# Retention of blocks 4 to 35 by chunks of 64 tokens, with quadrants of TensorE and a stacked operand for values and state

## The chip, the cores and the metric

The program runs on one core of a Trainium2 chip. A core has TensorE (PE in the profile: matmuls, with weight loads listed apart as PEld), VectorE (DVE), ScalarE (ACT), GpSimd (POOL) and SyncE (SP), which issues the DMA transfers here. Each engine runs its own instruction stream and waits for others by semaphores. The metric is the time of one execution on the device in microseconds (us); the time of a version is the median of several runs.

## The reference, cut to what matters

```python
# q, k, v: (8 batches, 8 heads, 576 tokens, 64)
scores = scale * np.matmul(q, k.transpose(0, 1, 3, 2))
gamma = 1.0 - 2.0 ** (-5.0 - np.arange(H))             # one decay for each head
Dmat = np.where(rel >= 0, gamma[:, None, None] ** rel[None, :, :], 0.0)   # rel = row - column
attn = np.matmul(scores * Dmat[None], v)
x = attn.transpose(0, 2, 1, 3).reshape(4608, 512)      # all heads of a token side by side
h = np.maximum(np.maximum(x @ w1, x @ w2), x @ w3)     # 512 -> 768, three times
out = h @ w_out                                        # 768 -> 512
```

The first part, retention, is linear attention with a decay: a block of tokens can be computed from scores within the block and from a state, the decayed sum of K^T V of all earlier tokens of the sequence, 64x64 for each head. The second part is a feed-forward network (FFN) with a maximum of three products.

## The kernel before

The 4608 tokens are 36 blocks of C = 128 tokens; four blocks make a tile of 512, and there are nine tiles. While the FFN of tile t runs, the retention of tile t + 1 is worked off between its products. The FFN of tile 0 is plain (its weights are being converted meanwhile). From tile 1 on, most of it is a fast matrix multiplication with fewer products and more additions: 20 products for each column block of 128 of the hidden layer (`up`), and seven for the output (`downs`). The names A to E are accumulating banks; a copy of the running sum is taken after most products.

A sequence has 576 tokens, four and a half blocks, so a block can hold the end of one sequence and the start of the next; masks with a zeroed corner and sliced operands take care of that. `start_of(g)` is the row at which a new sequence begins in block g.

The retention of a block (H = 8 heads, NP = 4 pairs of heads, D = 64; `half(j)` is partitions 64j to 64j + 63; `ps_r` is a pool of four PSUM banks):

```python
def decay_values(g):
    t = vds[g] = vpool.tile([C, H, D], FP32, tag="vd", name="vd")
    nc.gpsimd.tensor_tensor(t[:], raws.pop(("v", g))[:], gk[:].unsqueeze(2).to_broadcast([C, H, D]),
                            op=ALU.mult)
def transposes(g):
    both = qks[g] = {}
    if g >= BY_PE:
        for n in ("k", "q"):
            t = both[n] = att.tile([P, NP, C], FP32, tag=n + "T", name=n + "T", bufs=2 if n == "k" else 3)
            soon(partial(nc.vector.transpose, t[:].rearrange("a p c -> a (p c)"),
                         raws.pop(("kx" if n == "k" else n, g))[:].rearrange("a p b i -> a (p b i)")))
        return
    for n, src in (("k", raws["k", g]), ("q", raws.pop(("q", g)))):
        pool, tag = (ps_r, "r") if g >= CPT else (ps_x, "x")
        pt = pool.tile([P, NP, C], FP32, tag=tag, name=n + "t")
        for p in range(NP):
            nc.tensor.transpose(pt[:, p, :], pair(src, p), ident[:C, :C])
        t = both[n] = att.tile([P, NP, C], FP32, tag=n + "T", name=n + "T", bufs=2 if n == "k" else 3)
        nc.scalar.copy(t[:], pt[:])
def scores(g):
    chore(len(urgent))
    qT, kT = qks[g]["q"], qks[g]["k"]
    s = [ps_r.tile([C, NP, C], FP32, tag="r", name=f"s{j}") for j in range(2)]
    for p in range(NP):
        for j in range(2):
            r = slice(D * j, D * (j + 1))
            nc.tensor.matmul(s[j][:, p, :], lhsT=kT[r, p, :], rhs=qT[r, p, :], start=True, stop=True)
    st = sts[g] = att.tile([C, 2, NP, C], FP32, tag="st", name="st", bufs=2)
    for j in range(2):
        soon(partial(nc.vector.tensor_tensor, st[:, j], s[j][:],
                     masks[start_of(g)][:].unsqueeze(1).to_broadcast([C, NP, C]), op=ALU.mult))
def state(g):
    kr = raws["k", g]
    kvs[g] = None
    if begins(g):
        r = start_of(g) or 0
        kvs[g] = ps_r.tile([P, NP, D], FP32, tag="r", name="kv")
        for h in range(H):
            nc.tensor.matmul(kvs[g][half(h % 2), h // 2, :], lhsT=kr[r:, h, :], rhs=vds[g][r:, h, :],
                             start=True, stop=True)
def keep(g):
    def step(t, kv):
        if start_of(g) is not None:
            nc.vector.tensor_tensor(t[:], kv[:], gs[:], op=ALU.mult)
        else:
            nc.vector.tensor_tensor(t[:], kv[:], states[g][:], op=ALU.add)
            nc.gpsimd.tensor_tensor(t[:], t[:], gs[:], op=ALU.mult)
    if begins(g):
        t = states[g + 1] = stp.tile([P, NP, D], FP32, tag="state", name="state")
        soon(partial(step, t, kvs[g]))
def values(chunks, new_states=(), later=False):
    def before(g):
        return C if start_of(g) is None else start_of(g)
    chore(len(urgent))
    t, i = divmod(chunks[0], CPT)
    pool, tag = (ps_r, "r") if chunks[0] >= CPT - 1 else (ps_y, "y")
    o = [pool.tile([P, len(chunks), NP // 2, C], FP32, tag=tag, name="o") for _ in range(2)]
    for m, g in enumerate(chunks):
        for n in range(NP):
            for c in range(2):
                h = head(c, n)
                nc.tensor.matmul(o[n % 2][half(c), m, n // 2, :], lhsT=vds[g][:, h, :],
                                 rhs=sts[g][:, h % 2, h // 2, :], start=m == 0 and n < 2,
                                 stop=before(g) == 0, skip_group_check=True)
    for g in new_states:
        if g not in kvs:
            state(g)
    for m, g in enumerate(chunks):
        old = before(g)
        if old > 0:
            for n in range(NP):
                for c in range(2):
                    h = head(c, n)
                    r = half(h % 2)
                    nc.tensor.matmul(o[n % 2][half(c), m, n // 2, :old], lhsT=states[g][r, h // 2, :],
                                     rhs=qks[g]["q"][r, h // 2, :old], start=False, stop=True,
                                     skip_group_check=True)
    finish = partial(output, chunks, o, t, i)
    if later:
        return finish
    finish()
    for g in new_states[:1]:
        if g >= CPT:
            keep(g)
```

`soon` puts a step into a queue, `urgent`, that is worked off one step at a time between FFN products, so that VectorE and ScalarE work is spread. `chore(len(urgent))` empties it. When the steps of a tile are due is set here (twelve steps make a tile):

```python
for n in range(0, CPT, 2):
    a, b, m = CPT * t + n, CPT * t + n + 1, 6 * (n // 2)
    at(m, (keep, a), (transposes, b), (decay_values, b))
    ...
    at(m + 2, (scores, a), (scores, b))
    at(m + 3, (decay_values, a + 2))
    at(m + 4, (values, [a, b], [b, a + 2]), (transposes, a + 2), (load, a + 4))
```

The products of the FFN that surround the retention, with what ScalarE and VectorE do after each:

```python
PRODUCTS = """E a11 b12, E a14 b42, B s15 n5, A a22 b21, C s3 b23, B s19 b41, A s10 b32, C a13 b31, B s6 n2, A s13 b22,
              C a11 b11, B s14 n1, A s11 n4, D s7 b43, B a23 n6, A s20 b33, D s16 b13, B a21 n3, A a21 n8, A a24 n7"""
...
def up(t, h, fb):
    lo, hi = h[:, fb, 0:NH], h[:, fb, NH:NT]
    ps, of = {}, {}
    def join(out, a, b, op=ALU.add):
        nc.vector.tensor_tensor(out, a, b, op=op)
    def after(step):
        if step not in ("E1", "E2", "C2", "C3", "A6", "B5"):
            t = of[step] = ppool.tile([P, NH], FP32, tag="part", name="part")
            nc.scalar.copy(t[:], ps[step[0]][:])
        for out, ins, op in JOINS.get(step, ()):
            ins = [ps[n[0]] if n in ("E", "C") else of[n] for n in ins]
            join({"lo": lo, "hi": hi}.get(out) if out in ("lo", "hi") else of[out][:],
                 *(x[:] for x in ins), op)
    done = {}
    for chain, x, w in PRODUCTS:
        n = done[chain] = done.get(chain, 0) + 1
        if n == 1:
            pool, tag = (ps_x, "x") if chain in "AB" else (ps_y, "y")
            ps[chain] = pool.tile([P, NH], FP32, tag=tag, name=chain.lower())
        while x not in made[t]:
            chore()
        ends = n == sum(c == chain for c, _, _ in PRODUCTS)
        nc.tensor.matmul(ps[chain][:], lhsT=factor(w, fb), rhs=xS[t][x], start=n == 1, stop=ends,
                         skip_group_check=True)
        after(f"{chain}{n}")
        yield
...
            elif step % 2 or step % 5 == 4:
                chore(len(urgent) > 0)
```

## Time and profile before

| | |
|---|---|
| median of 3 runs | 775.69 us (775.1 to 776.63) |
| span of the profiled execution | 773.3 us |
| TensorE busy | 766.8 us, 99% |
| VectorE busy | 564.1 us, 73% |
| ScalarE busy | 325.9 us, 42% |
| GpSimd busy | 102.9 us, 13% |
| DMA | 59.33 MB, mean 77 GB/s |

The profile is of one execution. Its page gives each engine's busy time, the span in 40 slices, the DMA queues, the chain of work that ended last, and the costliest groups of instructions. Views of the trace show instructions in order of time: start in us, duration in us, engine, source line, operation, output and inputs by their names in the program, and in brackets how long the engine stood before it and what released it. An "x" and a number are instructions taken together. An fp32 matmul of the program is two records (MATMUL, with two LDWEIGHTS). Matmuls are pipelined, so durations overlap, and what a stretch costs is read from start to start. A shape as 64*128 before the output's is the part of the array that a product uses, rows by columns.

### The profile page before, as it was taken

Reading aid. Unit: us, or ns where it says so; the run is one execution under the profiler, and the core shown is the slowest. Engines: PE = TensorE matmul, PEld = TensorE weight load, DVE = VectorE, ACT = ScalarE, POOL = GpSimd, SP = SyncE. Lnnn points to the kernel's source line nnn. Section 1 sums busy time; section 2 is a strip of 40 time slices with the busy share of each in tenths; the row PEclk is TensorE's granted clock in tenths of the full one; section 3 lists DMA queues with packets and bytes.
Section 4 is the critical chain, followed back from the end, with each engine's and each line's share of the span. In section 5 each row is a group of like instructions: output and inputs, shape, how many; then the busy total and the mean of one; then the engine's idle time right before and its main releaser. Section 6 shows DMA issues by size and latency. Waiting matters only on the chain.

```text
span 773.3 us, 14511 instructions
## 1 busy us (share of the span) xinstructions
PE 766.8 (99%) x5032; PEld 626.5 (81%) x5032; DVE 564.1 (73%) x1249; ACT 325.9 (42%) x811; POOL 102.9 (13%) x124
## 2 busy tenths in 40 slices
PE   9999999999999999999999999999999999999998
PEld 8545454688888888888888888888888888888887
DVE  3898989799577856784768757876778568845672
ACT  3665631163254415451346234532544054514551
POOL 2210021111110201111111111110112001200000
PEclk9999999999999999999999999999999999999999
DMA  9995544333333332333233333333333323001001
GB/s 225 241 226 131 158 110 103 59 58 58 92 58 58 57 77 62 56 75 67 62 56 58 59 96 58 57 58 96 58 56 59 84 48 74 3 15 42 2 1 55
DMA packets 237083, 59.33 MB, mean 77 GB/s; under 512 B 217937, under 2 KB 235729, under 8 KB 237009
## 3 DMA queue, kind: packets, MB, share of 16 engines
q1 hardware_dynamic: 236432, 58.07, 34.9%
q8 instruction: 39, 0.64, 0.3%
q10 hardware_dynamic: 576, 0.33, 0.1%
q14 instruction: 36, 0.29, 0.1%
HBM read 48.89 MB, written 9.44 MB: 75 GB/s over the span
## 4 chain that ended last, share of the span: by engine, by line
PE 97%; SPq 1%; DVE 1%; DMA 1%; issue 0%; ACT 0%; DVEq 0%
PE a L588 18%; PE b L588 16%; PE dx L428 11%; PE up L611 11%; PE c L588 8%; PE dz L428 5%; PE d L588 5%; PE e L588 5%; PE s L243 4%; PE o L299 4%; PE down L598 3%; PE dy L428 3%; PE o L312 2%; PE kv L263 2%; SPq L210 1%; DMA qraw<-in_q_dram 1%
## 5 line engine op out<-in xcount | busy, mean ns | idle before, releaser
L568 DVE TENSOR_TENSOR part<-part 128x256 f32<-128x256 f32 x460 | 208.7, 462 | 78.2 <-ACT part L573 70.4
L573 ACT COPY part<-b 128x256 f32<-128x256 f32 x230 | 85.6, 372 | 126.0 <-PE b L588 114.6
L573 ACT COPY part<-a 128x256 f32<-128x256 f32 x276 | 102.7, 372 | 84.9 <-PE a L588 72.3
L214 POOL TENSOR_TENSOR vd<-vraw,gk 128x512 f32<-128x512 f32 x36 | 40.3, 1120 | 339.2 <-DMA vraw<-in_v_dram 219.9
L611 PE MATMUL up<-xT,w 128*128 128x512 f32 (+2 forms) x200 | 84.7, 578 | 0.3 <-DVE w L517 0.3
L588 PE MATMUL a<-s,w 128*128 128x256 f32 x276 | 82.3, 380 | 0.0
L588 PE MATMUL b<-s,n 128*128 128x256 f32 x276 | 82.1, 379 | 0.0
L611 PEld LDWEIGHTS up<-xT,w 128*128 128x128 f32 x200 | 36.8, 190 | 42.3 <-issue 39.2
L588 PEld LDWEIGHTS b<-s,n 128*128 128x128 f32 x276 | 52.4, 190 | 7.1
L588 PEld LDWEIGHTS a<-s,w 128*128 128x128 f32 x276 | 52.3, 190 | 7.3 <-issue 0.2
L588 PE MATMUL c<-xT,w 128*128 128x256 f32 x184 | 56.0, 386 | 0.0
L588 PE MATMUL b<-xT,n 128*128 128x256 f32 x184 | 55.4, 382 | 0.0
L588 PE MATMUL d<-s,w 128*128 128x256 f32 x184 | 55.1, 381 | 0.0
L568 DVE TENSOR_TENSOR h<-part 128x256 f32<-128x256 f32 x92 | 42.6, 463 | 6.6
L588 PE MATMUL e<-xT,w 128*128 128x256 f32 x184 | 47.3, 379 | 0.0
L588 PE MATMUL a<-xT,n 128*128 128x256 f32 x184 | 47.2, 379 | 0.0
L428 PE MATMUL dx<-To,H 128*128 128x256 f32 (+1 forms) x204 | 44.9, 370 | 0.0
L435 ACT COPY part<-dx 128x256 f32<-128x256 f32 (+1 forms) x34 | 10.5, 363 | 80.1 <-PE dx L428 77.9
L178 DVE TENSOR_TENSOR xT<-o,gq 128x512 f32<-128x512 f32 x28 | 18.1, 686 | 33.3 <-PE o L312 33.3
L428 PEld LDWEIGHTS dx<-To,H 128*128 128x128 f32 x204 | 36.6, 190 | 5.5 <-issue 1.0
L243 PEld LDWEIGHTS s<-qT,kT 64*128 64x128 f32 x576 | 33.9, 188 | 7.9 <-PE b L588 4.0
L272 POOL TENSOR_TENSOR state<-state,gs 128x256 f32<-128x256 f32 x24 | 18.6, 776 | 162.1 <-DVE state L271 162.1
(104 smaller groups left out, 1299.8 us busy)
## 6 DMA issues: line engine op xcount, KB each, us to landing
bits<-in_moe_w_dram SPq DMA_DIRECT2D x36, 256.0 KB, 5.6
out_dram<-osb SPq DMA_DIRECT2D x35, 256.0 KB, 2.1
kraw<-in_k_dram SPq DMA_DIRECT2D x32, 256.0 KB, 3.0
vraw<-in_v_dram SPq DMA_DIRECT2D x32, 256.0 KB, 3.4
qraw<-in_q_dram SPq DMA_DIRECT2D x464, 16.0 KB, 1.8
kxraw<-in_k_dram SPq DMA_DIRECT2D x464, 16.0 KB, 1.8
bits<-in_moe_w_out_dram SPq DMA_DIRECT2D x6, 512.0 KB, 4.7
qraw<-in_q_dram SPq DMA_DIRECT2D x6, 256.0 KB, 4.1
```

The lines of the kernel that those rows point to most:

```text
L178: (urgent or chores).popleft()()
L214: nc.gpsimd.tensor_tensor(t[:], raws.pop(("v", g))[:], gk[:].unsqueeze(2).to_broadcast([C, H, D]), op=ALU.mult)
L243: nc.tensor.matmul(s[j][:, p, :], lhsT=kT[r, p, :], rhs=qT[r, p, :], start=True, stop=True)
L263: nc.tensor.matmul(kvs[g][half(h % 2), h // 2, :], lhsT=kr[r:, h, :], rhs=vds[g][r:, h, :], start=True, stop=True)
L272: nc.gpsimd.tensor_tensor(t[:], t[:], gs[:], op=ALU.mult)
L299: nc.tensor.matmul(o[n % 2][half(c), m, n // 2, :], lhsT=vds[g][:, h, :], rhs=sts[g][:, h % 2, h // 2, :], start=m == 0 and n < 2, stop=be ...
L428: nc.tensor.matmul(o, lhsT=hS[n](fp)[:, m * P:(m + 1) * P], rhs=late["T"][n][:, fp, cols], start=first and fp == 0 and (m == 0 or last and ...
L568: nc.vector.tensor_tensor(out, a, b, op=op)
L573: nc.scalar.copy(t[:], ps[step[0]][:])
L588: nc.tensor.matmul(ps[chain][:], lhsT=factor(w, fb), rhs=xS[t][x], start=n == 1, stop=ends, skip_group_check=True)
L598: nc.tensor.matmul(b[:], lhsT=h[:, fb, m * P:(m + 1) * P], rhs=w_sb["out", fb], start=(fb == 0), stop=(fb == NF - 1))
L611: nc.tensor.matmul(ps[:, cols], lhsT=w_sb[i, fb][:, dc * P:(dc + 1) * P], rhs=xT[t][:, dc, cols], start=dc == 0 and cols.start == 0, stop= ...
```

## The change

Blocks 0 to 3 are computed as before. From block 4 on, a block is two chunks of 64 tokens, so that 576 tokens are nine chunks and a sequence begins only at a chunk's border.

- K^T V of a chunk and its scores are products of 64 by 64 with 64 columns: the four kinds (two chunks, K^T V or scores) fall into the four quadrants of TensorE's array, by the partitions in which operands and outputs lie. GpSimd scales K by the decay, where it scaled V before, and the decay of the scores is in the mask.
- V and the state are stacked: a tile `va` holds a chunk's 64 rows of V in one half of the partitions and the state before it in the other. A tile `m` holds the masked scores in one half and the transposed q in the other. One product of 128 rows then gives the values: 16 products with 64 columns a block, where there were 8 + 8 with 128 columns and the K^T V apart.
- V is loaded straight into its half of the stack. The running state is written into the other half of the next chunk's tile by VectorE (a sum of 64x512), by ScalarE where a sequence begins, and scaled by GpSimd at the end of a block.
- From block 7 on, the transposed q of both chunks comes out of one VectorE transpose into `m1`, and ScalarE copies the half that belongs to chunk 0 into `m0`. For blocks 4 to 6 TensorE transposes, and ScalarE copies the parts.
- Blocks of q and k for the transposes are loaded with all eight heads in one transfer, where two transfers took four heads each.

It is meant to cut TensorE's work for retention. The diff, cut to its core (cuts are marked; blank lines, the loads of V through the old path, the set-up of the first blocks and the schedule of tile 1 are left out):

```diff
             if 0 in blocks:
-                raws[n, g] = raw.tile([P, NP, C // 32, 32], FP32, tag=n, name=n + "raw", bufs=2)
+                raws[n, g] = raw.tile([P, H, 2, 32], FP32, tag=n, name=n + "raw", bufs=2)
             t = raws[n, g]
             for blk in blocks:
                 b, pos = divmod(g * C + 32 * blk, S)
-                for a in range(4):
+                c, e = divmod(blk, 2)
+                for a in range(2):
+                    r = D * (1 - c) + 32 * a
                     nc.sync.dma_start(
-                        t[32 * a:32 * a + 32, :, blk, :],
-                        src[b, a // 2::2, pos:pos + 32, 32 * (a % 2):32 * (a % 2) + 32].rearrange("p j i -> j p i"))
+                        t[r:r + 32, :, e, :],
+                        src[b, :, pos:pos + 32, 32 * a:32 * a + 32].rearrange("h p i -> p h i"))
+    def load_values(g):
+        for c in range(2):
+            t = stacked(g, c)
+            b, pos = divmod(g * C + D * c, S)
+            nc.sync.dma_start(t[half(c)], v[b, :, pos:pos + D, :].rearrange("h p d -> p h d"))
...
-    def decay_values(g):
-        t = vds[g] = vpool.tile([C, H, D], FP32, tag="vd", name="vd")
-        nc.gpsimd.tensor_tensor(t[:], raws.pop(("v", g))[:], gk[:].unsqueeze(2).to_broadcast([C, H, D]),
-                                op=ALU.mult)
+    def decay(g):
+        factor = gk[:].unsqueeze(2).to_broadcast([C, H, D])
+        if g < CPT:
+            t = vds[g] = vpool.tile([C, H, D], FP32, tag="va1", name="vd")
+            nc.gpsimd.tensor_tensor(t[:], raws.pop(("v", g))[:], factor, op=ALU.mult)
+            return
+        nc.gpsimd.tensor_tensor(raws["k", g][:], raws["k", g][:], factor, op=ALU.mult)
+        for c in range(2):
+            if place(g, c) == 0:
+                nc.gpsimd.memset(vas[g, c][half(1 - c)], 0.0)
...
     def transposes(g):
         both = qks[g] = {}
+        if g >= CPT:
+            kT = both["k"] = att.tile([P, H, D], FP32, tag="kT", name="kT", bufs=2)
+            m0, m1 = (att.tile([P, H, D], FP32, tag=f"m{c}", name=f"m{c}", bufs=3) for c in range(2))
+            ms[g, 0], ms[g, 1] = m0, m1
         if g >= BY_PE:
-            for n in ("k", "q"):
-                t = both[n] = att.tile([P, NP, C], FP32, tag=n + "T", name=n + "T", bufs=2 if n == "k" else 3)
-                soon(partial(nc.vector.transpose, t[:].rearrange("a p c -> a (p c)"),
-                             raws.pop(("kx" if n == "k" else n, g))[:].rearrange("a p b i -> a (p b i)")))
+            for n, t in (("kx", kT), ("q", m1)):
+                soon(partial(nc.vector.transpose, t[:].rearrange("a h c -> a (h c)"),
+                             raws.pop((n, g))[:].rearrange("a h b i -> a (h b i)")))
+            soon(partial(nc.scalar.copy, m0[half(1)], m1[half(1)]))
             return
...
+    def chunk_scores(g):
+        kT, kr = qks[g]["k"], raws.pop(("k", g))
+        sk = [ps_r.tile([P, H, D], FP32, tag="r", name=f"sk{j}") for j in range(2)]
+        for h in range(H):
+            for c in range(2):
+                if place(g, c) < S // D - 1:
+                    nc.tensor.matmul(sk[c][half(c), h, :], lhsT=kr[half(c), h, :], rhs=vas[g, c][half(c), h, :],
+                                     start=True, stop=True)
+            for c in (1, 0):
+                r = half(1 - c)
+                nc.tensor.matmul(sk[1 - c][half(c), h, :], lhsT=kT[r, h, :], rhs=ms[g, c][r, h, :],
+                                 start=True, stop=True)
+        def mask(c):
+            nc.vector.tensor_tensor(ms[g, c][half(c)], sk[1 - c][half(c)], gm[half(c)], op=ALU.mult)
+        def keep_chunk(c):
+            to = stacked(g + c, 1 - c)
+            if place(g, c) == 0:
+                nc.scalar.copy(to[half(c)], sk[c][half(c)])
+            else:
+                nc.vector.tensor_tensor(to[half(c)], sk[c][half(c)], vas[g, c][half(1 - c)], op=ALU.add)
+            if c:
+                nc.gpsimd.tensor_tensor(to[half(1)], to[half(1)],
+                                        gs_of[half(1)].unsqueeze(2).to_broadcast([D, H, D]), op=ALU.mult)
+        for c in range(2):
+            if place(g, c) < S // D - 1:
+                soon(partial(keep_chunk, c))
+            soon(partial(mask, c))
...
+                o = [pool.tile([P, 2, NP // 2, C], FP32, tag=tag, name="o")]
+                for m in range(2):
+                    for n in range(NP):
+                        for c in range(2):
+                            h = head(c, n)
+                            nc.tensor.matmul(o[0][half(c), n % 2, n // 2, half(m)], lhsT=vas[g, m][:, h, :], rhs=ms[g, m][:, h, :],
+                                             start=m == 0 and n == 0, stop=True, skip_group_check=True)
...
             a, b, m = CPT * t + n, CPT * t + n + 1, 6 * (n // 2)
-            at(m, (keep, a), (transposes, b), (decay_values, b))
+            at(m, (transposes, b), (decay, b))
             if a == 2 * CPT:
                 at(m, (load, a + 2))
-            at(m, (load, b + 2))
-            at(m + 2, (scores, a), (scores, b))
-            at(m + 3, (decay_values, a + 2))
-            at(m + 4, (values, [a, b], [b, a + 2]), (transposes, a + 2), (load, a + 4))
+            at(m + 2, (scores, a), (scores, b), (load, b + 2))
+            at(m + 3, (decay, a + 2))
+            at(m + 4, (values, a, b), (transposes, a + 2), (load, a + 4))
         return todo
```

## The prediction

> **What bounds the kernel now.** I read the page first: engine totals, then the slices, then the chain that ended last.

> ```profile
> PE 766.8 (99%) x5032; PEld 626.5 (81%) x5032; DVE 564.1 (73%) x1249; ACT 325.9 (42%) x811; POOL 102.9 (13%) x124
> ...
> PEclk9999999999999999999999999999999999999999
> ...
> PE 97%; SPq 1%; DVE 1%; DMA 1%; issue 0%; ACT 0%; DVEq 0%
> ```

> TensorE is busy for 99% of the span at full clock and carries 97% of the chain. In this state any TensorE work removed comes off the time, and any wait put on TensorE is added to it, because there is no slack there. VectorE at 73% has slack on average only.

> Next I read the timeline in a tile in the middle of the run. It shows what retention costs TensorE. First the scores of two chunks, and the first FFN product after them:

> ```profile
> 302.24 2.06 PE L243 MATMUL s<-qT,kT 64*128 64x128 f32 x32
> 304.23 0.70 PE L588 MATMUL c<-xT,w 128*128 128x256 f32 x2
> ```

> Start to start, the scores of a pair of blocks take 304.23 - 302.24 = 1.99 us. Then the values step of the same pair:

> ```profile
> 316.08 1.97 PE L299 MATMUL o<-st,vd 128*64 128x128 f32 x32
> 317.88 0.63 PE L263 MATMUL kv<-vd,kraw 128*64 128x64 f32 x16
> 318.44 1.10 PE L312 MATMUL o<-qT,state 64*64 64x128 f32 x32
> 319.47 0.70 PE L588 MATMUL b<-xT,n 128*128 128x256 f32 x2
> ```

> 319.47 - 316.08 = 3.39 us, with one K^T V left out at the end of a sequence. With both K^T V (1.03 us for 32 records, from 357.32 to 358.35 in the next pair) it is 1.80 + 1.03 + 1.03 = 3.86 us. I take 3.65 us as the mean of the 16 pairs. Every program matmul is two records here.

> [...]in the 64*128 form the 32 score records start 57 ns apart, and the first full product comes about 0.15 us later than that pace. [...]one copy that waits holds up all copies behind it. [...]The trace has 681 ns for 128x512[...]; I use 681 for 64x512 too.[...]

> **The change part by part, on TensorE.** Values: 16 products of 128x64 with 64 columns per block, 64 records a pair, of the same form as K^T V today. At 27.5 ns a record (16 records in 0.41 us from first to last start, 32 in 0.88) that is 1.76 us, and 0.15 us for the exit: 1.9 us. Against 3.65 us this saves 1.75 us a pair, 28 us in 16 pairs.

> Scores and K^T V: 32 products of 64x64 with 64 columns per block, four quadrants in turn, 128 records a pair (a few fewer at sequence ends). What a record costs is read from a pair in which 16 of 32 state records have 64 columns, against a block of 16 with 128 columns:

> ```profile
> 440.42 0.90 PE L312 MATMUL o<-qT,state 64*64 64x64 f32 x32
> 441.25 2.86 PE L428 MATMUL dx<-To,H 128*128 128x256 f32 x12
> ```

> ```profile
> 358.35 0.67 PE L312 MATMUL o<-qT,state 64*64 64x128 f32 x16
> 358.95 2.86 PE L428 MATMUL dx<-To,H 128*128 128x256 f32 x12
> ```

> 0.83 us less 0.60 us leaves 0.23 us for 16 records of 64 columns, 14.4 ns each. 128 x 14.4 = 1.84 us and 0.15 us exit make 2.0 us, what the scores cost now; for a longer run of records I allow +0.1 us a pair, 2 us in all. TensorE's own work thus falls by about **26 us**, and alone this would give 750 us.

> **VectorE, GpSimd, DMA.** The masks stay 64 instructions of 681 ns. 49 running sums (64x512, 681 ns, 33.4 us) replace some 28 of 409 ns (11.5 us): +22 us over 640 us. From 290.6 to 350.4 us, the FFN's up products, VectorE is busy for 45.8 of 59.8 us; four more microseconds fit. The scores of the second block of a pair do not wait for the sums of the first (the stack's halves are tracked apart), and the values come some 14 us after the scores, so this chain is hidden. GpSimd's scaling moves from V to K, 1.04 us as before. Q and K blocks come in half as many, twice as large transfers: hidden.

> **What is put on the path.** For each block from 7 on, VectorE transposes q into m1, and then ScalarE copies 64x512 of it to m0. In the changed program's ScalarE order these 29 copies stand amid the copies of FFN partial products, and TensorE's next product in the same bank waits for those. VectorE runs late just there, at the joins that end an FFN column block. For the third block of a tile, m0's copy stands directly ahead of the copy of the first b:

> ```profile
> 323.03 0.59 PE L588 MATMUL b<-s,n 128*128 128x256 f32 x2
> ...
> 323.66 0.37 ACT L573 COPY part<-b 128x256 f32<-128x256 f32 x1 [0.92 <-PE b L588]
> ...
> 324.33 0.59 PE L588 MATMUL b<-s,w 128*128 128x256 f32 x2
> ...
> 325.95 0.70 DVE L178 STREAM_TRANSPOSE qT<-qraw 128x512 f32<-128x512 f32 x1
> ```

> The transpose ends at 326.62 (the next VectorE instruction starts at 326.57). Now the copy of b at 323.66 has to wait for it: 326.62 + 0.05 + 0.61 (m0) + 0.37 (b) + 0.05 = 327.7, where the second b started at 324.33. **TensorE stands for 3.35 us.** VectorE's order from 321.48 on is the same before and after in this tile, so I take its time over.

> For the fourth block m0's copy stands behind the copy of c and ahead of that of the second b:

> ```profile
> 333.16 0.37 ACT L573 COPY part<-c 128x256 f32<-128x256 f32 x1
> ...
> 334.25 0.59 PE L588 MATMUL b<-s,n 128*128 128x256 f32 x2
> ...
> 335.25 0.42 DVE L269 TENSOR_TENSOR state<-kv,gs 128x256 f32<-128x256 f32 x1
> ...
> 336.54 0.67 DVE L178 STREAM_TRANSPOSE qT<-qraw 128x512 f32<-128x512 f32 x1
> ```

> The transpose ends at 337.2, less 0.33 for the state instruction that goes: 336.9. 336.9 + 0.05 + 0.61 + 0.37 + 0.05 = 337.95 against 334.25 for the third b: 3.7 us. The second block of a tile (transposed at its start, q at 374.92) gives 0.6 us in the same way, the first none, as ScalarE is idle then.

> The sum: third block 6 x 3.35 = 20 us (in the first Strassen tile the copy stands seven products ahead of the one that needs it, so I count none there), fourth block 7 x 3.7 = 26 us, second block 6 x 0.6 = 4 us, and 1 us for the copies of blocks 7 to 9: **50 us of waiting**. 775.7 - 26 + 50 = 800 us.

> **The rivals.** *The copies are harmless:* if VectorE reached the transposes 3 us sooner than in the old trace, the 26 us would show, 750 us. For it: fewer VectorE instructions stand in the pop order ahead of the fourth block's transpose. Against it: the joins that delay it wait for the last products of their column block and are unchanged, and the old trace has nothing idle between 321.48 and 326.62. *Quadrants at 64 columns do not keep 14 ns:* at 25 ns a record a pair costs 1.4 us more, 22 us in all, making 820 us with the waits and 772 without. Only one block of 16 records speaks for 14 ns. *VectorE becomes the bound:* a burst of eight 681 ns instructions (5.5 us) after the scores could delay the join that frees the bank of c. Counted from the scores' end, that join is done about 4.7 us later (with GpSimd's scaling between two sums), and the bank is needed after 5.6 us: it fits with 0.9 us to spare; if not, up to 1 us a pair more, 10 to 15 us.

> **Range and chances.** The two larger terms have opposite signs. The values' saving is safe to 3 us, the scores to 6 us, the waits to 10 us (a shift of 0.8 us in VectorE's lateness times 13 places). Together about 12 us: 784 to 815 us for 8 in 10. Slower by over 2% begins at 791.2 us, 9 us below the middle: 0.72. Faster by over 2% needs the waits to be nearly absent: 0.08. The rest, 0.20, is within 2%.

> **What would show it.** In the changed profile: values of a pair in 1.9 us and scores in 2.0 to 2.1 us start to start; in each tile two gaps of 3 to 4 us on TensorE, whose releaser is a ScalarE copy of b, with ScalarE idle before the m0 copy and its releaser VectorE's transpose of q. The waits of ScalarE on VectorE should rise by some 50 us, and TensorE's busy share fall to about 94%. If those gaps are under 1 us, the prediction fails, and the time is near 750 us; if the scores take 3 us or more, it fails upward.

## The result, and the profile after

The changed kernel takes **834.6 us** (median; 833.2 to 840.5) against 775.4 us (775.1 to 776.6) for the kernel before on the same chip: ratio 1.077, 95% interval 1.074 to 1.081. The direction was predicted, the size was not: 800 us was expected, 784 to 815 us allowed.

The page of the changed kernel, its engine totals and the granted clock in 40 slices:

```profile
PE 770.2 (93%) x6040; PEld 615.9 (74%) x6040; DVE 597.9 (72%) x1270; ACT 352.1 (42%) x869; POOL 121.8 (15%) x138
...
PEclk9999999999999999999998999999999999899999
```

TensorE's busy share fell from 99% to 93%, and the clock has two 8s where before it had none. Its mean is 0.973 of full speed. A clock of 0.973 over 831.5 us is some 45 us at half speed, or 22 us of work lost.

The waits by engine (time in all, times, longest, in us) name the stops:

```profile
ACT m L175 <- DVE m L175: 41.3, 20, 4.0
...
PE b L645 <- ACT part L630: 37.8, 21, 3.3
```

ScalarE waits 41.3 us with its copy m0<-m1 (recorded at line 175) for VectorE's transpose, and TensorE 37.8 us ahead of products of b for ScalarE's copies of b. One such place in the timeline (start, duration, what; in brackets the idle time before it and who ended it), third block of a tile:

```profile
339.72 0.59 PE L645 MATMUL b<-s,n 128*128 128x256 f32 x2
...
342.63 0.70 DVE L175 STREAM_TRANSPOSE m<-qraw 128x512 f32<-128x512 f32 x1
...
343.37 0.61 ACT L175 COPY m<-m 64x512 f32<-64x512 f32 x1 [3.94 <-DVE m L175]
344.01 0.37 ACT L630 COPY part<-b 128x256 f32<-128x256 f32 x1
...
344.43 0.70 PE L645 MATMUL b<-s,w 128*128 128x256 f32 x2 [3.26 <-ACT part L630]
```

Transpose, m0's copy, b's copy, next product of b: TensorE stood for 3.26 us. The product of b before it had ended at 340.31 us and ScalarE was idle from 339.43 us on, yet b's copy began at 344.01, behind m0's. Then something that the prediction does not have: of the products that follow, one starts at 346.21 and the next at 347.06 us, 0.85 us apart instead of 0.43. The table of stretches of 1 us (length, TensorE's busy time and instructions, **granted clock**, DMA share, GB/s) shows why:

```profile
344.00:345.00 1.00, 0.57 (x3) 1.00 0.33 51
345.00:346.00 1.00, 1.00 (x5) 0.72 0.39 60
346.00:347.00 1.00, 1.00 (x3) 0.50 0.48 73
...
349.00:350.00 1.00, 1.00 (x6) 1.00 0.46 71
```

The clock stays at 1.00 through this stop, falls to 0.50 a good microsecond after work has come back, and stays there for 3.4 us (the two stretches left out have 0.50 and 0.57). TensorE paid twice for this stop: in 3.26 us of idle time, and then in 3.4 us at half speed. The expectations below reckon with about 3.3 us at half clock after each stop, an estimate from this one.

Not every stop is followed by half clock. In this profile every stretch at half clock lasts 3.41 or 6.83 us, and all ten begin at multiples of 3.41 us from one another: they lie on one raster. Here are two stops of the same length, 3.26 us, from 254.96 and from 431.86 us on, in a table whose stretches are laid on that raster:

```profile
253.28:256.69 3.41, 1.68 (x8) 1.00 0.00 0
256.69:260.11 3.42, 1.89 (x9) 1.00 0.24 37
```

```profile
430.77:434.18 3.41, 1.09 (x6) 1.00 0.00 0
434.18:437.60 3.42, 2.48 (x6) 0.50 0.33 53
```

The first stop is split into 1.73 and 1.53 us of idle time, and the clock stays, in the stretch after these too. The second has 2.32 us in one stretch, and the clock is halved for the next two. In this profile each full-clock stretch of the raster with 2.13 us or more of idle time is followed by half clock, and none with 1.73 us or less; in number 4 below the border lies between 1.72 and 1.98 us. Elsewhere the border is not sharp: in number 10, of two stretches with 2.0 us of idle time each (ahead of b's products at 260.92 and 273.44 us), only the second is followed by half clock, and in the start of number 14 one with 1.00 us is (a stop of 1.09 us ends at 33.55 us; five records of 512 columns from 35.63 us on take 0.79 us each, the next eleven 0.43 us). This is read off the profiles; no run set the place of a stop on purpose.

To size both I added up TensorE's timeline, start to start, over five tiles (from the first dy product of the third tile to that of the eighth, dy being a bank of the output's products; in us; fourth and fifth column from experiments below):

| | before | changed | copies on GpSimd | before + copies |
|---|---|---|---|---|
| values, K^T V of before | 36.7 | 20.2 | 20.2 | 36.7 |
| scores, K^T V of changed | 19.9 | 20.6 | 20.4 | 19.8 |
| FFN's up products | 262.4 | 283.0 | 263.3 | 283.8 |
| FFN's down products | 91.6 | 91.9 | 91.9 | 91.6 |
| TensorE idle | 0.0 | 35.5 | 5.2 | 30.3 |
| sum | 410.6 | 451.1 | 400.9 | 462.2 |

The up products are the same instructions in every column. They take 20.6 us longer in the changed kernel. Of these tiles' ten stops over 2 us (five of 3.26, five of 2.32), eight are followed by half clock, 34.1 us in all; 31.8 us of it fall on up products and cost half of that, 15.9 us. The other 4.7 us come at full clock, around the waits: number 3 below, with 21 waits of up to 1.3 us and no half clock in these tiles, has 5.2 us of them. In these tiles +40.5 us = -16.5 (values) + 0.7 (scores) + 20.6 (up products: clock, and work around the waits) + 35.5 (idle) + 0.2 (down products). Ahead of the third tile the changed kernel is already 289.5 - 270.9 = 18.6 us late, partly by the first stops; the rest is the second question below.

### The profile page after: what moved, and what is told of

Read it like the earlier page. It is cut to its first block, busy times and chain, and to the rows that moved or that the text cites. A ratio compares the mean times of both kernels' runs of the same rounds, so it can differ in the third digit from the quotient of the medians.

```text
span 831.5 us, 16050 instructions
## 1 busy us (share of the span) xinstructions
PE 770.2 (93%) x6040; PEld 615.9 (74%) x6040; DVE 597.9 (72%) x1270; ACT 352.1 (42%) x869; POOL 121.8 (15%) x138
## 5 line engine op out<-in xcount | busy, mean ns | idle before, releaser
L630 ACT COPY part<-a 128x256 f32<-128x256 f32 x276 | 102.9, 373 | 76.6 <-PE a L645 67.2
L645 PE MATMUL b<-s,n 128*128 128x256 f32 x276 | 87.5, 400 | 17.1 <-ACT part L630 17.1
L645 PE MATMUL a<-s,w 128*128 128x256 f32 x276 | 86.6, 397 | 0.0
L310 POOL TENSOR_TENSOR va<-va,gs_of 64x512 f32<-64x512 f32 x28 | 30.7, 1097 | 329.6 <-DVE va L308 194.3
L645 PE MATMUL c<-xT,w 128*128 128x256 f32 x184 | 61.3, 417 | 2.8 <-ACT part L630 2.8
L645 PE MATMUL b<-s,w 128*128 128x256 f32 x92 | 30.1, 411 | 19.6 <-ACT part L630 19.6
L462 POOL TENSOR_TENSOR H<-h,H 128x256 f32<-128x256 f32 x24 | 18.4, 768 | 197.5 <-DVE H L461 174.3
L300 DVE TENSOR_TENSOR m<-sk,gm 64x512 f32<-64x512 f32 x64 | 44.0, 687 | 2.1 <-PE sk L296 0.6
L625 DVE TENSOR_TENSOR h<-part 128x256 f32<-128x256 f32 x92 | 39.1, 425 | 6.9
L645 PEld LDWEIGHTS c<-xT,w 128*128 128x128 f32 x184 | 36.8, 206 | 9.6 <-ACT part L630 3.5
L645 PEld LDWEIGHTS d<-s,w 128*128 128x128 f32 x184 | 35.3, 194 | 10.8 <-DVE part L625 5.9
```

Of the source, the lines that this page charges most:

```text
L300: nc.vector.tensor_tensor(ms[g, c][half(c)], sk[1 - c][half(c)], gm[half(c)], op=ALU.mult)
L310: nc.gpsimd.tensor_tensor(to[half(1)], to[half(1)], gs_of[half(1)].unsqueeze(2).to_broadcast([D, H, D]), op=ALU.mult)
L462: urgent.append(lambda: (pool(s3, a11, a21, op=ALU.subtract), pool(s4, a12, s2, op=ALU.subtract)))
```

## The experiments: is it the copy's wait?

My theory: ScalarE's copy of q, waiting for VectorE (3.94 us in the stop above), holds up the copies of FFN partial products behind it; TensorE stands (3.26 us), and its clock is halved afterwards (3.4 us). Rivals: VectorE's burst of masks and sums (A), the quadrant products themselves (B), ScalarE short of time (C). All ratios are to the kernel before on the same chip. The numbers are those of the kernels; a number 16 was not run.

**1. The copies on GpSimd.**

```diff
-            soon(partial(nc.scalar.copy, m0[half(1)], m1[half(1)]))
+            soon(partial(nc.gpsimd.tensor_copy, m0[half(1)], m1[half(1)]))
```

> The changed kernel, with the 29 copies of q (64x512, from m1 to m0) on GpSimd in place of ScalarE, in the same places of the order. Theory (a copy that waits for VectorE's late transpose holds up ScalarE's copies of FFN partial products, TensorE stands, and the granted clock is halved for about 3.3 us after each stop): the gaps of 2.1 to 3.3 us on TensorE whose releaser is ScalarE's copy of b go, about 41 us of the 61 us idle, the mean granted clock rises from 0.973 to 0.99 or more, some 20 us, and the time is 765 to 778 us. Rival A (VectorE with its eight masks and running sums after each pair of scores is the bound): TensorE waits for VectorE's joins instead, time 800 us or more. Rival B (the 128 quadrant records of a pair slow TensorE or its clock): gaps go but the clock stays under 0.98, time 790 to 800 us.

Measured: 776.8 us, ratio 1.0005 (0.9987 to 1.0022), clock 0.991. One line takes 58 us off. Its page:

```profile
PE 750.1 (97%) x6040; PEld 607.1 (78%) x6040; DVE 607.4 (78%) x1270; ACT 337.3 (44%) x840; POOL 140.9 (18%) x167
```

TensorE is busy for 97% again, with 770.2 - 750.1 = 20.1 us less: half clock fell from 44.4 to 13.7 us, and products at half clock count as busy for twice as long (0.85 us from start to start instead of 0.43), which makes some 15 us. What idle time is left in the five tiles (5.2 us) is mostly d waiting about 1 us for VectorE's join of e. So A is worth some 1 us a tile, and B nothing that shows.

**2. No copy: VectorE transposes q in two halves, straight into m0 and m1.**

```diff
-            for n, t in (("kx", kT), ("q", m1)):
-                soon(partial(nc.vector.transpose, ...whole tile...))
-            soon(partial(nc.scalar.copy, m0[half(1)], m1[half(1)]))
+            for t, x, r in ((kT, kx, slice(0, P)), (m1, qx, half(0)), (m0, qx, half(1))):
+                soon(partial(nc.vector.transpose, ...t[r] from x[r]...))
```

> The changed kernel without the copies of q: VectorE transposes q in two halves of 64 partitions, one straight into m0 and one into m1. VectorE gets 29 more instructions of about 0.67 us (19 us), ScalarE loses the 29 copies. Theory of the blocked copies: no ScalarE copy of b releases TensorE after 2 to 3 us any more, clock 0.99 or more, 765 to 785 us, the upper part if VectorE's 19 us delay the joins. Rival A (VectorE is the bound): as VectorE has more to do than in the changed kernel, 830 us or more.

Measured: 778.4 us, ratio 1.0018 (1.0005 to 1.0030). VectorE's busy time rises from 597.9 to 617.3 us, and the time falls by 56 us. Were VectorE the bound (A), it could not.

**3. The same ScalarE copies, put nine FFN products later into ScalarE's order** (a list counts down; the scores empty it).

```diff
-            soon(partial(nc.scalar.copy, m0[half(1)], m1[half(1)]))
+            soon(lambda: delayed.append([9, copy]))   # copy: the same instruction
```

> The changed kernel with the same 29 copies on ScalarE, each put into ScalarE's order nine FFN products (3.9 us) later, or ahead of the scores if these come sooner. ScalarE does the same work; only the place in its first-in-first-out order is another. Theory (the wait for the transpose, not the copy's 0.61 us, is the cost): when its turn comes the transpose is done, the gaps go, 765 to 780 us. Rival C (ScalarE lacks the time for the copies, or they are harmful in themselves): gaps as before, 820 to 835 us.

Measured: 784.2 us, ratio 1.0093 (1.0075 to 1.0112). ScalarE does all its work (352.6 us busy, 352.1 in the changed kernel); only the place differs, and 50 of the 59 us go. C falls. It is a little over the expected 780 us: the later copies give TensorE stops of up to 0.20 us at other products, and the up products of five tiles take 267.6 us instead of 263.3.

**4. The kernel before, with the copy alone** (qT's upper half onto itself, nothing else of the change).

```diff
+            soon(partial(nc.scalar.copy, both["q"][half(1)], both["q"][half(1)]))
```

> The kernel before, with one thing added: after each of the 29 VectorE transposes of q, ScalarE copies 64x512 of qT onto itself, in the place where the changed kernel copies m1 to m0. Nothing else of the change. Theory: 13 stops of TensorE as in the changed kernel, 6 of 3.3 us and 7 of 2.3 to 3.7 us, 36 to 46 us, and at half clock afterwards some 1.6 us each, 21 us: 830 to 845 us, clock 0.97. Rival C': the copies do no harm in the old order: 775 to 785 us; then it takes the change's VectorE load to make them late.

Measured: 843.3 us, ratio 1.084 (1.081 to 1.087), clock 0.970. ScalarE waits 37.8 us with the copy for VectorE's transpose. One stop in its timeline:

```profile
348.11 0.61 ACT L178 COPY qT<-qT 64x512 f32<-64x512 f32 x1 [3.94 <-DVE qT L178]
...
349.17 1.22 PE L589 MATMUL b<-s,w 128*128 128x256 f32 x2 [3.26 <-ACT part L574]
```

The same stop to the hundredth (later ones at this place take 3.16 us), in a kernel without quadrants, stacks or sums. 29 copies with 18 us of work in all, on an engine busy for 42% of the time, cost 66 us.

**8. The changed kernel with 83 products that nothing reads, in the places of the stops** (7 ahead of the product of b in a tile's third block, 5 in the fourth, 1 in the second).

```diff
+            for _ in range(fill[1]):
+                nc.tensor.matmul(idle[:], lhsT=ident[:], rhs=xS[t][x], start=True, stop=True)
```

> The changed kernel with 83 products more that nothing reads (128x128 by 256 columns, 0.43 us each, 36 us of work): 7 ahead of the product of b that stands 3.3 us in a tile's third block, 5 ahead of the one that stands 2.2 us in the fourth, 1 in the second. They run while TensorE would stand. Theory (each stop costs its idle time and then some 1.6 us more, because the clock is halved for about 3.3 us after it): idle time turns into busy time, the clock goes from 0.973 to 0.99, and though work is added the time falls by some 15 to 20 us, to 813 to 822 us. Rival (the lower clock has another cause, or costs nothing): 834 us, or up to 850 us.

Measured: 822.2 us, ratio 1.059 (1.057 to 1.062), clock 0.989. 36 us of useless TensorE work make the kernel 12.5 us *faster*. The stop in TensorE's timeline:

```profile
348.33 3.19 PE L657 MATMUL idle<-s,ident 128*128 128x256 f32 x14
351.75 0.70 PE L659 MATMUL b<-s,w 128*128 128x256 f32 x2 [0.23 <-ACT part L636]
352.28 0.59 PE L659 MATMUL a<-s,w 128*128 128x256 f32 x2
```

b still starts when ScalarE lets it, but the products behind it follow at full clock (a at 352.28, c at 352.71 us). Over five tiles the up products take 264.8 us (283.0 in the changed kernel), while stops and filling together take 38.2 us (35.5). These tiles have no half clock now. So the clock is its own term: some 18 us in five tiles, with what is lost around the waits. Number 10 below shows it another way: with the same idle time in these tiles (35.6 us), but 23.9 us at half clock in place of 34.1, its up products take 278.2 us in place of 283.0.

The five tiles became 15.6 us shorter (435.5 us), but the whole kernel gained 2.5 us less than the 15 us at which my range began. In the profile its third tile began 7.3 us later than in the changed kernel (296.8 against 289.5 us); 3.8 us of this are the five fillers of block 11, which ran from 187.31 to 191.15 us, behind the stop at 184.01 us and not in it.

## The experiments: where are the other 25 us?

Without the stops the kernel still only ties with before, although TensorE has some 25 us less work. The tiles do bring a gain: 400.9 against 410.6 us in five. The second tile's dy products, however, begin at 201.1 us instead of 188.4: **the first two tiles lose 12.7 us.** There VectorE and ScalarE convert the weights; in the kernel before VectorE is busy for 82.4 of the 88 us from 24 to 112 us, and TensorE waits 0.3 us for it.

**Places in memory (5, 6, 7, 9, 10, 12).** The first loads run slower in the changed kernel: 197 GB/s in the first 20 us against 225. The new tile gs_of (32 bytes in each partition) shifts all later tiles, which in the kernel before begin at multiples of 512 bytes. I moved tiles by resizing gs_of or the unused tile `fill`:

```diff
 5, 7:  gs_of = const.tile([P, 2 * H], ...)[:, :H]        # +64 bytes past a multiple of 512, not +32
 6:     FILL = 256   (224)                                # kernel before, +32
 12:    FILL = 352   (224)                                # kernel before, +128
 9, 10: gs_of ahead of fill, FILL = 192                   # multiples of 512 again
```

> The kernel before, with only the unused tile fill 32 bytes per partition larger (256 instead of 224), so that every later tile lies 32 bytes further on. Theory of the shift: transfers at the start fall from some 229 to 200 GB/s, FFN begins later, 779 to 788 us. Rival: an unused tile's size does nothing, 775 to 778 us.

> The kernel before with only the unused tile fill 128 bytes per partition larger, so that all later tiles begin 128 bytes past a multiple of 512. If the places matter to 512 bytes: 783 to 788 us, as with 32 bytes more (785.9). If a multiple of 128 bytes is enough: 775 to 777 us.

Measured: 6: 785.9 us, ratio 1.0129 (1.0110 to 1.0148); 12: 779.2 us, 1.0040 (1.0026 to 1.0055). The transfers' view of the first 20 us (count, KB each, median us from issue to landing), kernel before and then number 6:

```profile
kraw<-in_k_dram SPq DMA_DIRECT2D x4, 256.0 KB, 4.0
```

```profile
kraw<-in_k_dram SPq DMA_DIRECT2D x4, 256.0 KB, 5.3
```

The same loads of K take 4.0 us with tiles at multiples of 512, and 5.3 us 32 bytes past. At 128 past, the row has 5.0 us, yet that kernel lost 3.5 us where I expected 8 or more: these loads' time alone does not set the loss. In both, dy begins later, at 198.5 and 192.3 us.

> The first experiment's kernel (copies on GpSimd), with gs_of made 64 bytes per partition instead of 32, of which the first 32 are used. Every tile placed after gs_of lies 32 bytes further on, at the distance it had in the kernel before plus 64. Theory (the 32 bytes of gs_of shift the destinations of all later transfers, and this slows the start: 175 and 203 GB/s in the first two stretches of 10 us against 201 and 250 before, FFN begins 3 to 4 us later, V of block 4 and the last weights come late): transfers as fast as before, the dy products of the second tile begin 8 to 12 us sooner than at 201.1 us, and the time is 763 to 769 us. Rival (the order of the loads, or VectorE's work in the start): 773 to 778 us as before.

> The changed kernel with only gs_of made 64 bytes per partition. Theory of the shift: 8 to 12 us less than 834.6 us, 822 to 828 us; the stops of TensorE for ScalarE's copies and the clock after them stay. Rival: 833 to 838 us.

Measured: 5: 777.2 us, 1.0017 (1.0008 to 1.0026); 7: 837.7 us, 1.079 (1.076 to 1.082). Nothing gained: 64 bytes past, K still takes 5.0 us to land. No run has the tiles 256 bytes past, so whether a multiple of 256 would do is not shown.

> The first experiment's kernel (copies on GpSimd), with gs_of moved into the unused tile fill (gs_of first, then fill 32 bytes smaller), so that gq and all later tiles begin at multiples of 512 bytes in a partition, as in the kernel before. In the changed kernel they begin 32 bytes past one, in the fifth experiment 64 bytes past one. Theory (a transfer into places 32 or 64 bytes past a multiple of 512 bytes is slower): 220 to 230 GB/s in the first 20 us instead of 190, the second tile's dy products begin at 188 to 193 us instead of 201, and the time is 762 to 769 us. Rival (the start is late for another reason in the changed kernel): 775 to 778 us.

> The changed kernel with only gs_of moved into the unused tile fill, so that all later tiles begin at multiples of 512 bytes. Theory of the places: 8 to 14 us off the 834.6 us of the changed kernel, 820 to 827 us, with the stops of TensorE as they were. Rival: 833 to 838 us.

Measured: 9: 774.1 us, 0.9973 (0.9959 to 0.9986); 10: 834.3 us, 1.0752 (1.0728 to 1.0775). Here K lands in 3.9 us (number 9), but number 9 gains 2.7 us instead of 8 or more, and number 10 nothing. Loads were only the first of several waits in a row: with them faster, the 4.4 us that TensorE waited for V of block 4 in the changed kernel become, in number 10, one wait for GpSimd (0.71 us) and one for ScalarE (2.44 us), and TensorE stands 2.2 us for the last weights just as in the changed kernel. My theory of the places is true of the transfers and explains 2 to 3 us of the 12.7.

**11. Number 9 with VectorE's retention queue taken less often**, against the 1 us waits of d.

```diff
-                elif step % 2 or step % 5 == 4:
+                elif step % 2:
```

> The kernel with copies on GpSimd and the places of before, but the queue of VectorE's retention work is taken one item at every odd FFN step alone, no longer at every fifth too. Theory (the stops of about 1.0 us, one in each tile, where d waits for VectorE's join of e, come from the burst of eight masks and sums that pushes the joins back): spread further the burst lets the join through sooner, 3 to 6 us less than without, 758 to 764 us. Rival (the burst only moves to the flush ahead of the values, which then wait): 766 us or more.

Measured: 775.1 us, 0.9994 (0.9984 to 1.0004). The rival's time holds, but not its reason: the values of five tiles take 20.1 us as in number 9, so they don't wait. d waits 4.5 us in all (4.3 in number 9); what would shorten this stays open.

**13, 14, 15, 17, 18: who holds up the weights?** In number 9, VectorE's waits between 24 and 112 us are:

```profile
DVE mant L563 <- ACT mant L553: 3.7, 3, 2.0
DVE expo L568 <- ACT expo L558: 2.4, 4, 0.7
```

In the kernel before there were 0.4 us of these. ScalarE's share of the conversion stands behind 24 small copies of transposed k and q (64x256, 0.37 us each, 8.8 us; before 6 of 128x512, 3.5 us) and a copy of the carried state that waits 2.7 us for GpSimd.

```diff
 15:  carry():          nc.scalar.copy -> nc.gpsimd.tensor_copy           (number 9 and this)
 13:  also transposes as 16 products of 64x64 with the identity, then 3 copies of 512 columns, not 8 of 256
 17:  also key_masks() (gm, 2.4 us of GpSimd) right after decay(2)
 14:  kernel before, its 6 copies cut into 24 of 64x256
 18:  kernel before, 5 VectorE instructions of 64x512 more after the masks of blocks 4 to 7
```

> The kernel with copies on GpSimd and the places of before (774.1 us), with only the four copies of the carried state taken from ScalarE to GpSimd. Theory: half of the above, 771 to 773 us. Rival: 774 us.

> The kernel with copies on GpSimd and the places of before (774.1 us), with ScalarE relieved during the conversion of the weights: the transposes of blocks 4 to 6 are made as 16 products of 64x64 with the identity, which lands each chunk on its own half, so that 3 copies of 512 columns take the place of 8 copies of 256 (9 instead of 24, 5.1 us instead of 8.8), and the two copies of the carried state with the wait for GpSimd ahead of them (2.7 us) go to GpSimd. Theory (VectorE's conversion of weights, the bound of the first 110 us, waits 6.1 us for ScalarE's steps that stand behind these copies, and TensorE then for the weights): VectorE's waits for ScalarE between 24 and 112 us fall below 3 us, the second tile's dy products begin 3 to 6 us sooner than at 198.6 us, and the time is 767 to 771 us. Rival (VectorE's own added work, seven sums, delays the weights): 773 to 775 us.

> The kernel before, in which ScalarE brings the transposed k and q of blocks 4 to 6 out of PSUM in 24 copies of 64x256 in place of 6 of 128x512 (8.8 us instead of 3.5 us), as in the changed kernel. Theory of ScalarE holding up the conversion: VectorE waits 2 to 5 us more for ScalarE, TensorE stands for weights, and the time is 778 to 783 us. Rival: 775 to 777 us.

Measured: 15: 770.9 us, 0.9931 (0.9916 to 0.9946); 13: 771.3 us, 0.9938 (0.9923 to 0.9953); 14: 778.9 us, 1.0032 (1.0020 to 1.0045). The carried state's wait is worth 3 us. The small copies cost the kernel before 3 us, but taking them away on top of number 15 gave nothing, although VectorE's waits for ScalarE fell to 1.1 us: by then another wait was the last.

> The thirteenth run's kernel (771.3 us), with GpSimd's two products that make gm (2.4 us) put ahead of the scaling of V of block 3, where GpSimd waits 6 us for TensorE, instead of after it. In that kernel TensorE waits 2.2 us for GpSimd's scaling of K of block 4, which stands behind gm and the carried state. Theory: this wait goes, 768 to 770 us. Rival (VectorE's conversion of the weights sets the end of the start, so the time is lost again before the last weights): 771 us.

> The kernel before with five more VectorE instructions of 64x512 (0.68 us each, 3.4 us) after the masks of blocks 4 to 7, which leave the scores as they are: about what the changed kernel's seven sums add there, less the four states that go. Theory (VectorE is the bound of the conversion, so its added work delays TensorE there): 777 to 780 us. Rival (TensorE has that much slack to VectorE there): 775 to 776.5 us.

Measured: 17: **769.3 us**, 0.9911 (0.9895 to 0.9928); 18: 777.3 us, 1.0012 (1.0004 to 1.0019). Number 17 is the fastest kernel of the study, 0.9% ahead of before, with the change's whole computation. TensorE's wait for K's scaling is gone in it, but its interval overlaps that of number 13, and its dy products begin no sooner (196.4 against 196.2 us): what this step is worth, 2 us by the medians, is not settled. In 18, 3.4 us of VectorE work cost 1.0 us, so VectorE's added work alone explains little. Number 17's dy products are still 8 us behind the kernel before. These 8 us are not resolved into causes; its waits show 3.3 us for loads of q and 2.2 us for the last weights among them.

## Why the prediction went wrong

**TensorE's own work: right.** In the changed kernel's timeline, values of a pair and the product after them:

```profile
334.14 2.09 PE L375 MATMUL o<-m,va 128*64 128x64 f32 x64
336.16 0.70 PE L645 MATMUL b<-xT,n 128*128 128x256 f32 x2
```

Values 336.16 - 334.14 = 2.02 us (predicted 1.9); scores of the pair, from 320.27 to the next product at 322.29, also 2.02 us (predicted 2.0 to 2.1). By the table, (16.5 - 0.7) / 10 pairs x 16 = 25 us saved; predicted 26. One block of 16 records had been enough to size quadrants of 64 columns.

**The mechanism of the waits: right, one size off.** That a waiting copy holds up those behind it was my assumption; the stop that ends at 344.43 us shows it. 0.61 us for ScalarE's copy of 64x512 and 681 ns for VectorE's masks and sums of 64x512 were my estimates; the changed kernel's trace has 614 ns for 26 of the copies, 687 ns for the masks and 689 ns for the sums. The third block's stops were to be six of 3.35 us: six of 3.26. The second block's, six of 0.6 us: 0.48. The fourth block's, seven of 3.7 us: one of 2.75 (at c, in the first Strassen tile) and six of 2.1 to 2.3, some 10 us less in all. I had taken VectorE's old time less 0.33 us, so that q's transpose would end 336.9 - 334.25 = 2.65 us after the product was due; in the changed kernel such a transpose ended 1.26 us after it (m0's copy starts at 357.57 us, the product was due at 358.63 - 2.32 = 356.31). Waits for ScalarE's copies came to 37.8 + 2.8 us, predicted 50.

**The step that failed: "775.7 - 26 + 50".** It prices a stop at its idle time. After the stops the up products took 20.6 us longer in five tiles, 15.9 of them by half clock. In this trace half clock comes in stretches of 3.41 us, and the stretch ahead of it need not be idle all through: 2.13 us of idle time in it were enough, while 1.73 us were not. With the waits as measured and this term, 750 + 41 + 21, the sum would have been 812 us; the larger part of what is then missing is the start, below.

**The missing term: the start.** I followed ScalarE's copies through the tiles with the fast multiplication (the prediction's Strassen tiles) and did not look at the first two tiles, where VectorE's conversion of weights runs with ScalarE's help and TensorE's margin to it is small. It cost 12.7 us with the copies already on GpSimd. By the start of the second tile's dy products, the places in memory are 2.5 us of that (201.1 to 198.6 us) and the carried state's wait on ScalarE 2.0 us (to 196.6); some 8 us stay open. By the medians the two steps brought 2.7 and 3 us.

**The rivals.** "The copies are harmless" is refuted by number 4. "VectorE becomes the bound" was sized at 10 to 15 us and measured 4.3 us: four waits of about 1 us for VectorE's join, at d's bank and not at c's, for which I had reckoned a margin of 0.9 us. "Quadrants at 25 ns" is refuted by the scores' 2.02 us.

## What to carry to other kernels

Where TensorE is full, price a stop at its length plus what it costs afterwards (here 20.6 us for ten stops of 2.3 and 3.3 us, some of them without half clock), and look for it in the granted clock of short stretches. Before adding even a short copy to an engine's instructions, ask when its *input* is ready, and what stands behind it there: moving 29 short copies from ScalarE to GpSimd took 58 us off the changed kernel, and adding them on ScalarE cost the kernel before 66 us. If a stop can't be avoided, filling it with products that nothing reads can pay (12.5 us here).
